# Attention scores in two PSUM tiles instead of one, with a new instruction order

## The chip, the cores and the metric

The kernel runs on one core of a Trainium2 chip. The metric is device time in microseconds (us) of one execution. The core has five engines with queues of their own, each in order: TensorE (PE; its weight loads are shown as PEld), VectorE (DVE), ScalarE (ACT), GpSimd (POOL) and SyncE (SP, which issues the DMAs here). Semaphores order the work between them. Matmul results go to PSUM, which DVE and ACT read.

## The reference

Causal attention with a compressive memory, then a feed-forward layer; B = 4, H = 8, S = 576, D = 64, 2304 tokens, d_model 512, d_ff 2048:

```python
scores = scale * np.matmul(q, k.transpose(0, 1, 3, 2))     # causal, softmax
local = np.matmul(a, v)
mem_out = np.einsum('bhsd,bhde->bhse', q_p, M_prev) / mem_norm
out = g * mem_out + (1 - g) * local
x = out.transpose(0, 2, 1, 3).reshape(B * S, H * D)
h = x @ w_in
g = np.maximum(h, 0.0) + alpha * np.minimum(h, 0.0)
return (g @ w_out).astype(np.float32)
```

## The kernel before

The work is written as calls on five engine objects of a class `Work`. `add` (L212) does not issue an instruction: it records it with its dependencies on earlier ones, found from the regions that it reads and writes. For PSUM the region is a mask of 512-column banks, made by `banks` (L206), so that two accesses of one tile in different banks get no edge. `issue` (L389) then ranks all recorded instructions, adds biases by phase and engine from the table `STAGES` (L32), lays them out against a table of costs (`lay`, L319), and issues them in the order of their planned starts, each on its engine's queue. The framework under the kernel sets the semaphores from that order and from the tiles that the instructions touch; the kernel has no say in them. All instructions go through one line, L417 (two matmuls issued as a pair: L242 and L243).

Queries come in five blocks of rows: 64 rows of all four batches together at first (batch "Z"), then four blocks of 128 rows of each batch, i = 1 to 4, each of which sees 64 + 128 i keys. A unit is one head with two blocks: a narrow unit has i = 1 and 2 (192 and 320 columns of scores), a wide one i = 3 and 4 (448 and 576). Per batch there are 8 narrow units and then 8 wide ones. A unit's scores are matmuls into PSUM (`unit_scores`, L959; in batches 1 to 3 two fp16 matmuls for each piece of up to 512 columns, with qT and then with qS, into the same place; 576 goes as 512 and 64). DVE reads each block once, with mask, scale and row maximum (`lowest`: E<-s, which also writes mx), ACT takes the exponential, `unit_probs` scales, splits into two fp16 parts (P) and transposes by DMA to PT, and `pair_values` multiplies with v into the tile bank. In batch 0 scores are fp32: `first_pair` (L930) runs two heads at once as paired matmuls, and the probabilities of narrow units are turned by TensorE in `unit_probs`, four blocks at a time, copied out by ACT (PT<-s). Between all of these TensorE runs the MoE matmuls (h for x @ w_in, y for g @ w_out), which make up most of its time; after the last unit it runs them alone.

PSUM has eight banks: one for the tile bank, two each for h and y, and three in one tile SS (name s in the profile) for scores:

- batch Z's scores and values, and the narrow units of batches 1 to 3 (both blocks in one bank): the next of three banks, by `third`
- wide units of batches 1 to 3: 448 in the first bank, 576 in the second and third
- batch 0: narrow pairs in the first two banks, one head each; turned blocks in the third; wide pairs with 448 in the third and 576 in the first two

Of the kernel before, what the change touches and what calls it, by code (L numbers as in the profile page):

```python
# [33 lines left out]
        "A0": -271.6, "A:DVE": -630.1, "BK0": 128.2, "BK:ACT": 57.8, "C0": -243.2, "C1": 111.2, "C2": -388.2,  # L34
        "C3": -1232.9, "C:ACT": 6.9, "C:DVE": -1010.6, "C:PE": -155.1, "I:DVE": 74.2, "I:POOL": 455.7,
# [9 lines left out]
        "P:DMA": -611.7, "P:DVE": -1203.9, "P:PE": -63, "P:POOL": 139.7, "S0": 5563.1, "S1": -1561.9, "S3": -1827.9,  # L45
        "S:ACT": 91.8, "S:DVE": 248, "V0": -1.2, "V:PE": -55.7, "a0": -645.8, "a1": -2.3, "a2": -2, "a3": 458.7,
        "a4": 395.9, "a:ACT": -1239, "a:DVE": -1609.6, "bk0": -153.9, "bk1": 135.1, "bk2": -2.6, "bk3": -1.5,
        "bk:ACT": -1438.9, "bk:DMA": -473.7, "bk:DVE": -477.6, "bk:PE": -584.5, "bv0": 174, "bv1": 65.7, "bv2": 2.6,
# [5 lines left out]
        "o31": -1071.1, "o33": -466.4, "o:ACT": -431.9, "o:DMA": 29.3, "o:DVE": -726.2, "o:PE": -469.3, "oZ": -11.6,  # L54
        "oZ:ACT": -1559.9, "oZ:DVE": -1291.2, "oZ:PE": -81.7, "p1": -2914.9, "p2": -286.9, "p3": -715.7, "p4": 13.8,
        "p:ACT": -1229.2, "p:DVE": -633.5, "q1": 61.7, "q2": -1110, "q3": 59, "q:ACT": -234.1, "q:DVE": -671.8,
# [7 lines left out]
        "y:DVE": -1121.7, "y:PE": 639.6,  # L64
    }),
# [4 lines left out]
        "C:ACT": -20.6, "C:DVE": -11.7, "C:PE": 37.9, "I": 6.7, "I:POOL": 1.3, "J": 1.8, "J:ACT": -11.3,  # L70
# [12 lines left out]
        "P33:DVE": 1.3, "P33:POOL": 14.4, "P:ACT": -9.2, "P:DMA": -16.7, "P:DVE": -12.2, "P:PE": 14.4, "P:POOL": 4.9,  # L83
# [6 lines left out]
        "bk:ACT": -23.9, "bk:DMA": 2, "bk:DVE": -13.2, "bk:PE": 28.8, "bv0:ACT": -10.3, "bv0:DVE": -13, "bv1": -0.4,  # L90
# [83 lines left out]
class Work:  # L174
# [31 lines left out]
    def banks(self, ap):  # L206

        (ps, pn), *free = ap.ap
        o = ap.offset % ps
        return (2 << (o + sum(st * (n - 1) for st, n in free)) // 512) - (1 << o // 512)  # L210
# [210 lines left out]
def kernel(  # L421
# [24 lines left out]
    NP = H // 2  # L446
# [28 lines left out]
    def third():  # L475
        turns[0] += 1
        return SS[:, turns[0] % 3 * 512:turns[0] % 3 * 512 + 512]
# [979 lines left out]
```

## Time and profile before

| | us |
|---|---|
| median of 3 runs (584.89 to 585.94) | 585.43 |
| the profiled execution | 584.66 |
| its span, first to last instruction | 582.8 |
| TensorE busy | 541.5 |
| DVE busy | 456.0 |
| ACT busy | 380.7 |

The mean granted clock of TensorE is 0.972 of 2.4 GHz. The profile shows, per engine, when each instruction ran, how long the engine sat idle before it, and which other engine's instruction released it ("<-"). Names are the program's, out<-in: s is the tile SS, E the scores after DVE, mx the row maxima.

### The profile page before, as it was taken

How to read it: one execution, taken by the hardware profiler on the slowest of the kernel's cores; microseconds unless marked ns; L12 is line 12 of the kernel's file. 1: busy time of each engine (PE TensorE's matmuls, PEld its weight loads, DVE VectorE, ACT ScalarE, POOL GpSimd, SP SyncE). 2: the span in 40 equal slices, each digit the busy share in tenths (PEclk: the TensorE clock that was granted, in tenths of full speed). 3: DMA queues.
4: the chain of work that ended last, by engine and by line, in shares of the span. 5: the costliest groups of instructions: out<-in, count | busy, mean ns of one | idle time of the engine just before them, and what ended most of it. 6: DMA issues, size and time to landing. Idle time of an engine off the chain costs nothing.

```text
span 582.8 us, 12013 instructions
## 1 busy us (share of the span) xinstructions
PE 541.5 (93%) x4421; PEld 356.6 (61%) x4421; DVE 456.0 (78%) x1197; ACT 380.7 (65%) x790; POOL 81.6 (14%) x142
## 2 busy tenths in 40 slices
PE   9558999799999999989899999999999899999997
PEld 4347644364566676647666767587666666766663
DVE  4898899789999899999999999989887664322331
ACT  3466696658989468978788787886886653322322
POOL 2000310031420021211222120221221110000000
PEclk9759999799999999999999999999999999999999
DMA  7899738563489795476998838788545470100000
GB/s 254 197 342 237 208 94 244 193 165 82 91 162 204 175 219 121 99 164 153 207 231 186 177 100 162 162 181 160 105 87 103 126 157 14 47 1 1 36 1 36
DMA packets 226026, 82.84 MB, mean 142 GB/s; under 512 B 216224, under 2 KB 216240, under 8 KB 225968
## 3 DMA queue, kind: packets, MB, share of 16 engines
q1 hardware_dynamic: 225968, 82.09, 60.1%
q8 instruction: 34, 0.56, 0.4%
q14 instruction: 24, 0.20, 0.1%
HBM read 35.66 MB, written 5.77 MB: 71 GB/s over the span
## 4 chain that ended last, share of the span: by engine, by line
PE 62%; DVE 16%; ACT 8%; issue 5%; DMA 5%; POOL 2%; SPq 2%; POOLq 0%; DVEq 0%; ACTq 0%
PE y L417 24%; PE h L417 24%; PE s L417 7%; PE bank L417 4%; DVE E L417 4%; DVE P L417 3%; POOL E L417 2%; DMA E<-in_moe_w_in_dram 2%; SPq L417 2%; DVE r L417 2%; DVE gg L417 1%; DVE R L417 1%; ACT r L417 1%; PE s L242 1%; ACT q L417 1%
## 5 line engine op out<-in xcount | busy, mean ns | idle before, releaser
L417 PE MATMUL h<-x,R 128*128 128x256 f16 x1536 | 256.2, 273 | 1.5 <-DVE r L417 1.4
L417 PE MATMUL y<-R,gg 128*128 128x512 f16 (+1 forms) x832 | 254.3, 397 | 1.3 <-ACT t L417 0.7
L417 PE MATMUL bank<-v,PT 128*128 128x64 f16 x1224 | 190.4, 193 | 0.1
L417 PEld LDWEIGHTS <-R 128*128 128x128 f16 x1536 | 148.8, 98 | 38.0 <-issue 6.3
L417 PEld LDWEIGHTS <-PT 128*128 128x128 f16 x1224 | 118.2, 98 | 19.3 <-issue 14.9
L417 PEld LDWEIGHTS <-gg 128*128 128x128 f16 x768 | 74.7, 98 | 76.6 <-issue 1.3
L417 POOL TENSOR_SCALAR E<-q,nrm,sm 128x64 f32<-128x64 f32 x112 | 69.0, 630 | 277.8 <-DVE sm L417 173.4
L417 ACT ACTIVATE E<-E,mx 128x320 f32<-128x320 f32 (+3 forms) x136 | 81.0, 601 | 30.1 <-DVE mx L417 26.1
L417 DVE SCALAR_TENSOR_TENSOR P<-E,mx,P 128x384 f16<-128x384 f32 (+3 forms) x112 | 75.4, 699 | 5.9 <-ACT P L417 5.3
L417 DVE SCALAR_TENSOR_TENSOR r<-r,oma,h 128x256 f32<-128x256 f32 x128 | 56.6, 475 | 26.8 <-ACT r L417 26.6
L417 ACT ACTIVATE P<-E,mx 128x384 f16<-128x384 f32 (+3 forms) x112 | 70.6, 673 | 10.0 <-POOL E L417 7.9
L417 ACT ACTIVATE r<-h 128x512 f32<-128x512 f32 x72 | 41.9, 589 | 50.7 <-PE h L417 29.1
L417 DVE SCALAR_TENSOR_TENSOR gg<-r,gsc,gg 128x512 f16<-128x512 f32 x56 | 41.8, 747 | 40.6 <-ACT gg L417 31.5
L417 DVE CUSTOM_DVE_ANT_0 E<-s,mask,pm 128x320 f32<-128x320 f32 (+3 forms) x96 | 57.4, 611 | 11.0 <-PE s L417 9.2
L417 ACT ACTIVATE gg<-r,gsc 128x512 f16<-128x512 f32 x56 | 40.0, 716 | 38.3 <-PE y L417 36.1
L417 PE MATMUL s<-k,qT 128*128 128x64 f16 (+5 forms) x136 | 36.4, 294 | 5.9 <-DVE mx L417 5.6
L417 PE MATMUL s<-k,qS 128*128 128x192 f16 (+4 forms) x120 | 32.7, 294 | 5.9 <-DVE mx L417 5.9
L417 PE MATMUL h<-R 128*128 128x256 f32 x128 | 31.4, 386 | 2.3 <-ACT R L417 1.9
L417 PEld LDWEIGHTS h<-R 128*128 128x128 f32 x128 | 22.9, 190 | 8.8 <-ACT R L417 2.7
L417 ACT ACTIVATION_READ_ACCUMULATOR E<-E,mx 128x1 f32 x124 | 23.3, 188 | 0.0
L417 ACT ACTIVATE R<-R,wsc 128x1024 f16<-128x1024 f32 x16 | 18.3, 1143 | 7.5 <-PE h L417 3.6
L417 ACT ACTIVATE t<-y,u 128x512 f32<-128x512 f32 x18 | 12.2, 680 | 13.2 <-PE y L417 13.0
(183 smaller groups left out, 628.5 us busy)
## 6 DMA issues: line engine op xcount, KB each, us to landing
q<-in_q_dram SPq DMA_DIRECT2D x16, 256.0 KB, 4.2
vn<-in_v_dram SPq DMA_DIRECT2D x16, 256.0 KB, 4.1
out_dram<-t SPq DMA_DIRECT2D x16, 256.0 KB, 2.3
kn<-in_moe_w_in_dram SPq DMA_DIRECT2D x6, 512.0 KB, 6.6
kn<-in_moe_w_out_dram SPq DMA_DIRECT2D x6, 512.0 KB, 4.7
kn<-in_k_dram SPq DMA_DIRECT2D x12, 256.0 KB, 3.9
qS<-qT SPq DMA_DIRECT2D x24, 128.0 KB, 2.6
R<-in_moe_w_in_dram SPq DMA_DIRECT2D x4, 512.0 KB, 6.6
```

The lines of the kernel that those rows point to most:

```text
L242: first[1](*first[2], **first[3])
L417: fn(*a, **kw)
```

## The change

SS becomes two tiles: s1 of one bank and s2 of two banks. The banks that are used are the same number; where they lie:

- batch Z and the narrow units of batches 1 to 3 alternate between s1 and the first bank of s2 (`other` in place of `third`)
- wide units of batches 1 to 3: 448 in s1, 576 in s2
- batch 0: narrow pairs in s2, turned blocks in s1; wide pairs with 448 in s1 and 576 in s2

`banks` goes; in the plan every access to a PSUM tile now counts as an access to the whole tile. The functions s1, s2, s3 are renamed, since the names are used for tiles. All values in STAGES are new, and so is the order that `issue` makes from them. The instructions are otherwise the same.

```diff
--- before.py
+++ after.py
@@ -31,106 +31,108 @@
 STAGES = [
     (2, {
-        "A0": -271.6, "A:DVE": -630.1, "BK0": 128.2, "BK:ACT": 57.8, "C0": -243.2, "C1": 111.2, "C2": -388.2,
-        "C3": -1232.9, "C:ACT": 6.9, "C:DVE": -1010.6, "C:PE": -155.1, "I:DVE": 74.2, "I:POOL": 455.7,
...
+        "A0": 10.6, "A:DVE": 50.6, "BK0": 102.5, "BK:ACT": -27.7, "BK:PE": 3.4, "C0": -56.4, "C1": 22.3, "C2": 335.8,
+        "C3": -920, "C:ACT": 1096.2, "C:DVE": -3.8, "C:PE": -943.6, "I": -699.2, "I:DVE": 79.2, "I:POOL": 497.7,
...
@@ -203,12 +205,6 @@
         m, size = self.known[key], ps * w
         return sum(m << size * h for h in range(2) if p0 < 64 * (h + 1) and p0 + pn > 64 * h), size
 
-    def banks(self, ap):
-
-        (ps, pn), *free = ap.ap
-        o = ap.offset % ps
-        return (2 << (o + sum(st * (n - 1) for st, n in free)) // 512) - (1 << o // 512)
-
     def add(self, kind, engine, name, a, kw):
         outs = [kw[x] for x in ("out", "accum_out") if kw.get(x) is not None]
         rest = list(a) + [x for n, x in kw.items() if n not in ("out", "accum_out")]
@@ -223,7 +219,7 @@
         for x, write in [(x, False) for x in ins] + [(x, True) for x in outs]:
             if x.tensor.name in self.fixed:
                 continue
-            m = self.banks(x) if x.space == PSUM else self.cells(x)[0]
+            m = 1 if x.space == PSUM else self.cells(x)[0]
             wrote, read = self.state.setdefault(x.tensor.name, ([], []))
             deps.update(o for o, c in wrote if c & m)
             if not write and x.space == PSUM:
@@ -469,12 +465,13 @@
 
     bank = psp.tile([128, 512], F32, tag="bank")
     o_sc = bank[:, 256:512]
-    SS = psp.tile([128, 1536], F32, tag="s")
+    s1 = psp.tile([128, 512], F32, tag="s1")
+    s2 = psp.tile([128, 1024], F32, tag="s2")
     turns = [0]
 
-    def third():
+    def other():
         turns[0] += 1
-        return SS[:, turns[0] % 3 * 512:turns[0] % 3 * 512 + 512]
+        return (s1, s2[:, 0:512])[turns[0] % 2]
     ident = cp.tile([128, 128], F32, name="ident")
     ones = cp.tile([128, 128], F32, name="ones")
     mask = cp.tile([128, 576], F32, name="mask")
@@ -936,8 +933,8 @@
             for a in range(2):
                 i = bl[j if bl[0] == 1 else a ^ j ^ 1]
                 w = 64 + 128 * i
-                o = 512 * a + 192 * j if bl[0] == 1 else 1024 if i == 3 else 0
-                cols.append((a, i, SS[:, o:o + w]))
+                o = 512 * a + 192 * j if bl[0] == 1 else 0
+                cols.append((a, i, (s1 if i == 3 else s2)[:, o:o + w]))
             cols.sort(key=lambda x: -x[2].shape[1])
             for c0 in (0, 512):
                 for n, (a, i, row) in enumerate(cols):
@@ -966,10 +963,10 @@
         width = [64 + 128 * i for i in bl]
         es, mx, sm = unit_tiles(b, h, bl)
         if bl[0] == 1:
-            ps = third()
+            ps = other()
             where = [ps[:, 0:width[0]], ps[:, width[0]:sum(width)]]
         else:
-            where = [SS[:, 0:width[0]], SS[:, 512:512 + width[1]]]
+            where = [s1[:, 0:width[0]], s2[:, 0:width[1]]]
         qT, qS, k1, _ = stacks[b, h // 2]
         for i, w, s in zip(bl, width, where):
             for c0 in range(0, w, 512):
@@ -1003,7 +1000,7 @@
             PT = wkp.tile([128, 9, 128], F32, tag="PT", bufs=TB)
             for c0 in range(0, ns, 4):
                 c1 = min(c0 + 4, ns)
-                pt = SS[:, 1024:1024 + 128 * (c1 - c0)]
+                pt = s1[:, 0:128 * (c1 - c0)]
                 for c in range(c0, c1):
                     T.transpose(pt[:, (c - c0) * 128:(c - c0) * 128 + 128], E[:, c * 128:c * 128 + 128], ident)
                 A.copy(PT[:, c0:c1].rearrange("p s c -> p (s c)"), pt)
@@ -1092,7 +1089,7 @@
                              (n["k"][t], [(ps, kT[ps, a]) for a, ps in enumerate((slice(0, 64), slice(64, 128)))], "y")):
             flipped([x[:, 2 * a:2 * a + 2].rearrange("p h d -> p (h d)") for a in range(NP)],
                     [(ps, o.rearrange("p n c -> p (n c)")) for ps, o in outs], tag)
-        s = third().rearrange("p (h n) -> p h n", h=H)
+        s = other().rearrange("p (h n) -> p h n", h=H)
         for h in range(H):
             for c in (slice(0, 64), slice(64, 128)):
                 T.matmul(s[c, h, :], lhsT=qT[:, h // 2, c], rhs=kT[:, h % 2, h // 2, c], start=True, stop=True)
@@ -1120,7 +1117,7 @@
         (V if OZ[0] else G).tensor_tensor(E, E, sm[:, :, None].to_broadcast([128, H, 64]), op=ALU.mult)
         PT = wkp.tile([128, H, 128], F32, tag="PT", bufs=TB)
         flipped([P[:, h] for h in range(H)], [(slice(0, 128), PT.rearrange("p h c -> p (h c)"))], "hy"[t])
-        o = third().rearrange("p (a n) -> p a n", a=NP)
+        o = other().rearrange("p (a n) -> p a n", a=NP)
         for h in range(H):
             a, ps = h // 2, slice(64 * (h % 2), 64 * (h % 2) + 64)
             for b in range(2):
@@ -1276,13 +1273,13 @@
     V.tensor_scalar(xsc, ra[:, 0, 0:1], XS * 2.0 ** -15, None, op0=ALU.mult)
     V.tensor_scalar(isa, ra[:, 1, 0:1], 2.0 ** 15, None, op0=ALU.mult)
 
-    def s1(u):
+    def scores(u):
         unit_scores(*u)
 
-    def s2(u):
+    def probs(u):
         unit_probs(*u)
 
-    def s3(u):
+    def values(u):
         b, h, bl = u
         if h % 2 == 1:
             if h == 1:
@@ -1305,7 +1302,7 @@
     def tick():
         t = done[0]
         done[0] += 1
-        for f, lag in ((s3, LAG), (s1, 0), (s2, 1)):
+        for f, lag in ((values, LAG), (scores, 0), (probs, 1)):
             if 0 <= t - lag < len(units) and units[t - lag]:
                 f(units[t - lag])
         do(bulk[:BULK])
```

## Rows read from the trace of the kernel before

**Rows 1.** The page: busy time by engine; the chain that ended last, by engine and line.
```profile
PE 541.5 (93%) x4421; PEld 356.6 (61%) x4421; DVE 456.0 (78%) x1197; ACT 380.7 (65%) x790; POOL 81.6 (14%) x142
...
PE 62%; DVE 16%; ACT 8%; issue 5%; DMA 5%; POOL 2%; SPq 2%; POOLq 0%; DVEq 0%; ACTq 0%
PE y L417 24%; PE h L417 24%; PE s L417 7%; PE bank L417 4%; DVE E L417 4%; DVE P L417 3%; POOL E L417 2%; DMA E<-in_moe_w_in_dram 2%; SPq L417 2%; DVE r L417 2%; DVE gg L417 1%; DVE R L417 1%; ACT r L417 1%; PE s L242 1%; ACT q L417 1%
```

**Rows 2.** Windows: length; busy us (count) of PE, PEld, DVE, ACT, POOL; clock; DMA share, GB/s.
```profile
0.00:60.00 60.00, 42.91 (x286) 28.75 (x288) 47.43 (x126) 31.00 (x77) 4.22 (x13) 0.80 0.92 257
60.00:120.00 60.00, 54.21 (x241) 29.78 (x242) 51.72 (x160) 43.10 (x106) 7.89 (x16) 0.94 0.63 187
...
180.00:480.00 300.00, 286.67 (x2793) 198.45 (x2790) 268.49 (x715) 228.09 (x478) 52.49 (x96) 1.00 0.73 155
480.00:583.00 103.00, 99.14 (x706) 63.62 (x703) 31.81 (x62) 29.66 (x46) 0.00 (x0) 0.99 0.07 22
```

**Rows 3.** Waits of the whole span: us in total, times, longest.
```profile
PE s L417 <- DVE mx L417: 11.5, 22, 0.8
...
DVE E L417 <- PE s L417: 9.4, 17, 1.0
...
PE s L417 <- ACT PT L417: 2.4, 4, 0.8
```

**Rows 4.** Timeline, TensorE, 248 to 262: start, duration, instruction, [idle before, releaser].
```profile
250.25 0.35 PE L417 MATMUL s<-k,qS 128*128 128x448 f16 x1 [0.64 <-DVE mx L417]
...
254.38 0.35 PE L417 MATMUL s<-k,qT 128*128 128x448 f16 x1
...
261.91 0.19 PE L417 MATMUL s<-k,qS 128*128 128x64 f16 x1 [0.75 <-DVE mx L417]
```

**Rows 5.** Timeline, DVE, the same stretch.
```profile
249.37 0.82 DVE L417 CUSTOM_DVE_ANT_0 E<-s,mask,pm 128x576 f32<-128x576 f32 x1
...
254.78 0.82 DVE L417 CUSTOM_DVE_ANT_0 E<-s,mask,pm 128x576 f32<-128x576 f32 x1 [0.41 <-PE s L417]
...
261.17 0.68 DVE L417 CUSTOM_DVE_ANT_0 E<-s,mask,pm 128x448 f32<-128x448 f32 x1 [0.44 <-PE bank L417]
```

**Rows 6.** Chain of waits, 248 to 262: start, us, what.
```profile
249.37 0.82 DVE E L417
```

**Rows 7.** Groups by form: count, busy us, mean ns, idle before, releasers.
```profile
L417 PE MATMUL s<-k,qS 128*128 128x448 f16 x24 | 8.4, 352 | 3.3 <-DVE mx L417 3.3
...
L417 PE MATMUL s<-k,qT 128*128 128x64 f16 x24 | 4.6, 192 | 2.9 <-DVE mx L417 2.9
...
L417 PE MATMUL s<-k,qS 128*128 128x64 f16 x24 | 4.6, 192 | 1.5 <-DVE mx L417 1.5
...
L417 PE MATMUL s<-k,qS 128*128 128x512 f16 x24 | 9.1, 379 | 0.8 <-DVE mx L417 0.8
...
L417 PE MATMUL s<-k,qS 128*128 128x320 f16 x24 | 7.0, 299 | 0.3 <-DVE mx L417 0.3
```

**Rows 8.** Tile s, 188 to 214; then timeline of TensorE and DVE to 224.
```profile
L417 PE MATMUL s<-k,qT x8: 246/272/300, 191.8 to 213.7; 128*128 128x192 f16 x4, 128*128 128x320 f16 x4
L417 PE MATMUL s<-k,qS x8: 244/272/300, 191.9 to 209.7; 128*128 128x192 f16 x4, 128*128 128x320 f16 x4
L417 DVE CUSTOM_DVE_ANT_0 E<-s,mask,pm x6: 413/480/550, 200.9 to 212.9; 128x320 f32<-128x320 f32 x3, 128x192 f32<-128x192 f32 x3
...
213.66 0.25 PE L417 MATMUL s<-k,qT 128*128 128x192 f16 x1
...
222.37 0.30 PE L417 MATMUL s<-k,qT 128*128 128x320 f16 x1 [0.31 <-DVE mx L417]
...
221.78 0.53 DVE L417 CUSTOM_DVE_ANT_0 E<-s,mask,pm 128x320 f32<-128x320 f32 x1
...
222.95 0.42 DVE L417 CUSTOM_DVE_ANT_0 E<-s,mask,pm 128x192 f32<-128x192 f32 x1 [0.63 <-PE s L417]
```

**Rows 9.** Timeline, TensorE, a transpose of batch 0's turned blocks.
```profile
86.82 0.33 PE L417 MATMUL s<-ident,E 128*128 128x128 f32 x1 [0.68 <-ACT PT L417]
```

More of the change, by code (lines that the diff above doesn't have):

```diff
@@ L33 @@
     (2, {
-        "A0": -271.6, "A:DVE": -630.1, "BK0": 128.2, "BK:ACT": 57.8, "C0": -243.2, "C1": 111.2, "C2": -388.2,
-        "C3": -1232.9, "C:ACT": 6.9, "C:DVE": -1010.6, "C:PE": -155.1, "I:DVE": 74.2, "I:POOL": 455.7,
[9 rows of a table removed]
-        "P:DMA": -611.7, "P:DVE": -1203.9, "P:PE": -63, "P:POOL": 139.7, "S0": 5563.1, "S1": -1561.9, "S3": -1827.9,
-        "S:ACT": 91.8, "S:DVE": 248, "V0": -1.2, "V:PE": -55.7, "a0": -645.8, "a1": -2.3, "a2": -2, "a3": 458.7,
-        "a4": 395.9, "a:ACT": -1239, "a:DVE": -1609.6, "bk0": -153.9, "bk1": 135.1, "bk2": -2.6, "bk3": -1.5,
@@ L48 @@
-        "bk:ACT": -1438.9, "bk:DMA": -473.7, "bk:DVE": -477.6, "bk:PE": -584.5, "bv0": 174, "bv1": 65.7, "bv2": 2.6,
[5 rows of a table removed]
-        "o31": -1071.1, "o33": -466.4, "o:ACT": -431.9, "o:DMA": 29.3, "o:DVE": -726.2, "o:PE": -469.3, "oZ": -11.6,
-        "oZ:ACT": -1559.9, "oZ:DVE": -1291.2, "oZ:PE": -81.7, "p1": -2914.9, "p2": -286.9, "p3": -715.7, "p4": 13.8,
-        "p:ACT": -1229.2, "p:DVE": -633.5, "q1": 61.7, "q2": -1110, "q3": 59, "q:ACT": -234.1, "q:DVE": -671.8,
[7 rows of a table removed]
-        "y:DVE": -1121.7, "y:PE": 639.6,
+        "A0": 10.6, "A:DVE": 50.6, "BK0": 102.5, "BK:ACT": -27.7, "BK:PE": 3.4, "C0": -56.4, "C1": 22.3, "C2": 335.8,
@@ new lines @@
+        "C3": -920, "C:ACT": 1096.2, "C:DVE": -3.8, "C:PE": -943.6, "I": -699.2, "I:DVE": 79.2, "I:POOL": 497.7,
+        "J:ACT": 470.6, "J:DVE": 108, "J:PE": -179.3, "K": 47.5, "K:POOL": 2.3, "L0K": -713.8, "L0K:DMA": 228.2,
[6 rows of a table added]
+        "LW:DMA": 605.3, "LZ": 27.3, "LZ:DMA": -1145.9, "Lz": 8.5, "Lz:DMA": -8.6, "N": 87.9, "N:PE": 292.5,
+        "P01": 4, "P03": 3.7, "P11": 777.2, "P13": 823.4, "P21": 168.1, "P23": 236.6, "P31": -675.3, "P33": -247.2,
+        "P:ACT": 988.7, "P:DMA": 668.5, "P:DVE": -882.6, "P:PE": -157.8, "S0": 4737.2, "S1": -1253, "S3": -2953.6,
@@ new lines @@
+        "S:ACT": -87.5, "S:DVE": 168.1, "V0": -874.8, "V:DVE": 211.2, "V:PE": -90.8, "a0": 5.7, "a1": 46.8,
+        "a2": -161.5, "a3": 389.6, "a4": -42.9, "a:ACT": -265.2, "a:DVE": 239.4, "bk0": -173.5, "bk1": 344.8,
+        "bk2": 244.5, "bk3": 3.1, "bk:ACT": -687.5, "bk:DMA": 246.9, "bk:DVE": 1380.7, "bk:PE": 100.3, "bv0": -0.7,
[5 rows of a table added]
+        "o31": 144.8, "o33": 10.1, "o:ACT": -779.8, "o:DMA": 580.1, "o:DVE": -613.6, "o:PE": 33.3, "oZ": 10.8,
[5 rows of a table added]
+        "v:DVE": 634.9, "v:PE": 331.4, "x0": -121.5, "x:ACT": 2.1, "x:DVE": 73.7, "y0_10": -412.5, "y0_11": -68.6,
@@ L65 @@
+        "y0_30": 187.3, "y0_31": 1834.4, "y1_10": -18.1, "y1_11": 103.3, "y1_30": -419.6, "y1_31": 103.8,
+        "y2_10": 184.2, "y2_11": 220.2, "y2_30": -3073.8, "y2_31": -122.6, "y3_10": 764.1, "y3_11": 98,
+        "y3_31": 447.3, "y4_11": -1599.1, "y:ACT": -1231.1, "y:DMA": 642.8, "y:DVE": -750.7, "y:PE": 1282.7,
     }),
     (1, {
[3 rows of a table removed]
-        "C:ACT": -20.6, "C:DVE": -11.7, "C:PE": 37.9, "I": 6.7, "I:POOL": 1.3, "J": 1.8, "J:ACT": -11.3,
[12 rows of a table removed]
-        "P33:DVE": 1.3, "P33:POOL": 14.4, "P:ACT": -9.2, "P:DMA": -16.7, "P:DVE": -12.2, "P:PE": 14.4, "P:POOL": 4.9,
[6 rows of a table removed]
@@ L90 @@
-        "bk:ACT": -23.9, "bk:DMA": 2, "bk:DVE": -13.2, "bk:PE": 28.8, "bv0:ACT": -10.3, "bv0:DVE": -13, "bv1": -0.4,
[12 rows of a table removed]
-        "h4_11:DVE": -11.2, "h4_11:PE": 46.8, "h:ACT": -8.7, "h:DVE": -12.2, "h:PE": 45.7, "n": 4, "n:PE": 0.2,
[5 rows of a table removed]
-        "o33:PE": 1.8, "o:ACT": -22.9, "o:DMA": -16.1, "o:DVE": -13.2, "o:PE": 46, "oZ": 3.1, "oZ:ACT": 0.2,
[9 rows of a table removed]
-        "s33:PE": 48.3, "s:ACT": 6, "s:DVE": -12.2, "s:PE": 45.5, "sZ": 7.1, "sZ:DVE": -0.4, "sZ:PE": 0.3,
[13 rows of a table removed]
-        "y:DVE": -11.7, "y:PE": 45.5,
[3 rows of a table added]
+        "C3:PE": -8.9, "C:ACT": 13.2, "C:DVE": 9.3, "C:PE": -17.2, "I": -57.9, "I:POOL": -8.6, "J:ACT": -18.7,
[6 rows of a table added]
@@ new lines @@
+        "LW3": -8.7, "LW3:DMA": -22.1, "LW:DMA": -2.8, "LZ:DMA": -42.6, "Lz:DMA": -4.4, "N": 0.9, "N:PE": -13.7,
[5 rows of a table added]
+        "P33:DMA": -3.8, "P33:DVE": -7.4, "P33:POOL": -37, "P:ACT": 15, "P:DMA": -20.1, "P:DVE": 8.9, "P:PE": -86.4,
[21 rows of a table added]
+        "h4_11:PE": -16.7, "h:ACT": 10, "h:DVE": 8.9, "h:PE": -16.3, "n": -27.5, "n:PE": -9.4, "o01": -15,
[5 rows of a table added]
+        "o33:DVE": 21.3, "o33:PE": -55.2, "o:ACT": -0.5, "o:DMA": -50.1, "o:DVE": 13.1, "o:PE": -18, "oZ": -97,
[4 rows of a table added]
+        "q:ACT": 39, "q:DVE": 9.7, "r0:ACT": 0.9, "r0:DVE": 9.9, "r:ACT": 35.7, "r:DVE": 13.6, "s01:ACT": -1.2,
[4 rows of a table added]
@@ L134 @@
+        "s33:ACT": 1.7, "s33:PE": -49.1, "s:ACT": 12.1, "s:DVE": 8.9, "s:PE": -16.3, "sZ": 8.1, "sZ:ACT": 98.3,
[14 rows of a table added]
+        "y4_11:PE": -16, "y:ACT": 21.9, "y:DMA": 2.5, "y:DVE": 8.4, "y:PE": -16.3,
     }),
```

159 rows, old and new, of the table STAGES are left out of this document.

## The prediction

> **What bounds the kernel now.** I read the page first. TensorE is busy 541.5 of 582.8 us, and it has 62% of the chain that ended last; DVE has 16%, and its reads of the scores (DVE E) are 4% of the span [rows 1]. So an idle microsecond of TensorE counts nearly in full, as long as its backlog of MoE matmuls only moves forward. Second, the windows by stretch say where TensorE idles: 17.1 us in 0 to 60 (60 less 42.91), 5.8 in 60 to 120, 13.3 in 180 to 480 and 3.9 in 480 to 583, the last a stage in which it runs almost alone [rows 2]. From 180 us on the granted clock is 1.00, the 2.4 GHz level, so time saved there has no second price in clock. Third, the waits: "PE s <- DVE mx" is 11.5 us in 22 waits, by far the largest wait of TensorE, and on the other side DVE waits 9.4 us in 17 pieces for score matmuls [rows 3].
>
> What these 11.5 us are is the core of the case. A wide unit writes 448 columns into bank 0 and 576 (512 and 64) into banks 1 and 2 of the one tile SS. DVE starts reading the 576 at 249.37 for 0.82 us [rows 5]; the second matmul of the 448, in another bank, starts only at 250.25, after 0.64 us of idle, put down to that read [rows 4]. The first matmul of the same 448 columns has already run, so bank 0 was free: nothing in the data asks for this wait. The other direction shows too: at 254.38 TensorE begins another first matmul of a 448, which lasts 0.35, and DVE's read of the 576 starts at 254.78, 0.05 after its end, with 0.41 of idle [rows 4, 5]. A third pair is the 448 read at 261.17 and the 64-column matmul at 261.91, 0.75 late. The semaphores therefore go by tile here, not by bank. The chain of waits runs through such a read (0.82 us of DVE at 249.37), so it is on the path [rows 6]. The planner of before does not know: its `banks` gives accesses in different banks no edge, so it lays the matmul beside the read and the chip puts it behind.
>
> **The Trainium skill against the trace.** "PSUM — Partial Sum Buffer", section "PSUM bank collisions raise a hardware error", says that engines on different banks run clean and that a guard by bank is enough. By this rule the three banks of SS need no waits between them, splitting the tile would save nothing, and the sum would stay at the time before. The measurement differs: the 448's matmul waited 0.64 us on a read in other banks [rows 4, 5]. I go by the rows; the rule's outcome is a rival below.
>
> **The change, part by part.**
>
> *Wide units of batches 1 to 3.* The blocks keep their banks' count, but lie in two tiles, s1 (448) and s2 (512 and 64). Waits between them go. By form of matmul, TensorE's idle time before 448 of qS is 3.3, before 64 of qT 2.9, before 64 of qS 1.5, before 512 of qS 0.8 and before 320 of qS 0.3 us [rows 7]: 8.8 us. All of these are later matmuls of a block whose first one has been written, so their own place was free. I count all as saved. The other 2.7 us (11.5 less 8.8) stand before first matmuls, which may have to wait for a read of their own place; I take half, 1.3, with ends 0 and 2.7. DVE's 9.4 us of waiting for scores [rows 3] also shrink, at no price: DVE has 31.5 us of idle time in 180 to 480 [rows 2], so when TensorE moves forward by 10 us there, DVE is still not full. I add nothing for it, since TensorE sets the end.
>
> *Narrow units of batches 1 to 3.* Before, they rotate over three banks, after over two tiles, with the second bank of s2 unused. This is the change's cost. In 188 to 214 us four pairs of 320-column matmuls are done, and two more units have begun (the last at 213.66), while DVE has read three units [rows 8]. The sixth unit thus stands in the place of the third. In a rotation of two it has to wait for the fourth's reads, which end at 223.37: 9.7 us later. So the third place is used, and up to 18 units (six of eight in each batch) are pushed back. But DVE's reading is what is late: the scores of such a unit lie unread for many microseconds, and what was written early was not read earlier. Queued behind a score matmul on TensorE are the MoE matmuls, which have nothing to do with it; the new order, whose planner has the two tiles as they are, can put them in front. The cost is bounded below by 0 (a gain beyond that is in the sum already) and above by both reads of a unit, 0.53 and 0.42 us [rows 8], for all 18: 17.1 us. The nearest measured case of a narrow score behind a read is 0.31 us at 222.37 [rows 8]. I take that for every third unit: 6 x 0.31 = 1.9 us.
>
> *Batch 0.* Narrow pairs write both banks of s2 as they wrote banks 0 and 1, and turned blocks have one bank as before. The wait of transposes for ACT's copies, 2.4 us [rows 3], as 0.68 at 86.82 [rows 9], is a true one between two users of one bank, and stays. That pairs and turned blocks no longer wait for each other is worth little: no PE wait of that kind over 0.3 us is among the rows I found. 0, with 1 as the end. The wide pairs write 448 and 576 together; a pair needs both reads either way: 0. Scores and values of the first blocks go from three places to two, and each use is read before the next but one: 0.
>
> *`banks` removed, `m = 1`.* This adds edges only in the plan, where the chip has waits already. It costs no instruction. Renamed functions: 0.
>
> *New order.* Same instructions, other queue order on every engine, SP's loads and POOL's included. The trace of before can't show it. I bound it by idle time that an order can win or lose: TensorE's 17.1 + 5.8 us before 120 us [rows 2]. A quarter of that either way is 5.7 us; I take 0, as the loads and warm-up that fill this stage are the same.
>
> **Sum.** The profiled execution took 584.66 us (582.8 of span, 1.9 around it), 0.77 below the median of 585.43. 584.66 - 8.8 - 1.3 + 1.9 = 576.5; with 0.77 that is 577.2 us at the median, 1.4% less. With the order's 5.7 either way: 571.5 to 582.9.
>
> **Rivals.**
>
> *The wait is not the tile's (same).* If the semaphores go by bank, and the rows show a chance meeting of waits, the split saves nothing and the time is 585.4, give or take 1. Against it: three pairs within 13 us, each ending within 0.15 us of the other engine's instruction, in both directions [rows 4, 5]. Likewise if DVE becomes the bound and takes all back. Against that: its 31.5 us of idle time. Together 0.13.
>
> *Two places for narrow scores bind (slower).* The place is the narrow stage of batches 1 to 3, where TensorE stands before a score, with MoE matmuls queued behind, until DVE has read the unit before the last. At the full price, 585.4 - 8.8 + 17.1 = 593.7. It decides from 8.8 / 18 = 0.49 us a unit on: below, the change still gains. For it: the third place is in use throughout [rows 8]. Against it: TensorE waited only 0.31 where it met such a read, and the planner sees the two tiles. 0.13.
>
> *More than the false waits (faster still).* If the first matmuls' waits go too and the order wins half of the idle time in 60 to 120: 585.4 - 11.5 - 2.9 = 571.0. 0.12.
>
> The forecast holds the remaining 0.62.
>
> **How the numbers follow.** Time 577.2. The range must reach the order's ends and the case without a saving: 570 to 586 leaves out the slow rival and the far end of the fast one, under 0.2 together. Within 0.2% means 584.3 to 586.6, about what a measurement of this kernel can tell from none. Faster: 0.62 + 0.12 + 0.04 (the part of the first rival in which a little is left) = 0.78; same 0.09; slower 0.13.
>
> **What would show it.** Right: "PE s <- DVE mx" falls from 11.5 to 3 us or less, no 448 or 64 of qS or 64 of qT waits for DVE any more, TensorE's idle time in 180 to 480 falls from 13.3 to about 5, and a read of 576 runs beside a 448 matmul. The buffers' price shows as waits before narrow 192-column first matmuls, each ended by DVE; over 0.49 us on average means the slow rival. Wrong: the same waits at the same places (waits not by tile); or idle time that moves ahead of 120 us or to "PE bank <- DMA" and "PE h <- DVE" (new order); or waits gone and the end unmoved, with DVE without idle time in 180 to 480.

## The result and the profile after

The changed kernel takes 562.77 us (median of 4 runs, 561.1 to 564.0) against 585.16 before: a ratio of 0.961, 95% interval 0.959 to 0.964, so 22.4 us less. The forecast was 577.2, its range 570 to 586; the direction held, the time lies below the range. Its profiled execution took 562.94 us, 561.1 of it span; before, 584.66 and 582.8.

The page of the changed kernel, to be read against [rows 1]: busy time by engine, and the chain that ended last by engine and by line.

```profile
PE 533.8 (95%) x4421; PEld 353.8 (63%) x4421; DVE 452.7 (81%) x1197; ACT 377.9 (67%) x790; POOL 84.8 (15%) x142
...
PE 54%; DVE 8%; DMA 5%; issue 2%; ACT 1%; POOL 0%; POOLq 0%; DVEq 0%
PE y L413 24%; PE h L413 22%; PE bank L413 4%; PE s L413 4%; DMA PT<-P 4%; DVE P L413 2%; DVE E L413 1%; DVE q L413 1%; DVE r L413 1%; DMA k<-k 1%; DVE nrm L413 1%; DVE t L413 1%; DVE gg L413 1%; DMA x<-xn 1%; ACT P L413 0%
```

TensorE works the same 4421 matmuls in 7.7 us less (541.5 to 533.8) and is idle 14.0 us less (582.8 less 541.5 is 41.3; 561.1 less 533.8 is 27.3). The chain's shares add up to 70% of the span here and to all of it before, so they can't be set beside each other as they stand; of the part that was followed DVE has 8 in 70, and its reads of scores (DVE E) 1 in 70, against 16 and 4 in 100 before.

The windows of the changed kernel, with the columns of [rows 2]:

```profile
0.00:60.00 60.00, 46.88 (x314) 30.73 (x315) 48.83 (x137) 34.82 (x87) 4.27 (x13) 0.89 0.93 257
60.00:120.00 60.00, 59.17 (x271) 34.76 (x268) 58.58 (x174) 47.42 (x113) 13.65 (x20) 1.00 0.69 195
120.00:180.00 60.00, 58.97 (x511) 36.57 (x510) 58.66 (x133) 53.48 (x91) 11.62 (x13) 1.00 0.60 134
180.00:480.00 300.00, 291.37 (x2813) 202.78 (x2811) 261.69 (x707) 219.16 (x465) 55.23 (x96) 0.99 0.73 153
480.00:562.00 82.00, 77.36 (x523) 48.94 (x519) 24.92 (x49) 22.97 (x36) 0.00 (x0) 0.99 0.06 22
```

Idle time of TensorE by stretch, before to after: 17.1 to 13.1 in 0 to 60, 5.8 to 0.8 in 60 to 120, 13.3 to 8.6 in 180 to 480. So 9.0 of the 14.0 us of idle time that went lay ahead of 120 us, where my sum had 0; and there the granted clock rose from 0.80 to 0.89 and from 0.94 to 1.00, between the levels of 1.2 and 2.4 GHz.

What TensorE waits for now (us in total, times, longest), the four longest:

```profile
PE bank L413 <- DVE stv L413: 4.8, 1, 4.8
PE bank L413 <- DMA PT<-P: 4.7, 5, 1.4
PE h L413 <- DVE P L413: 3.4, 1, 3.4
PE h L413 <- DMA x<-xn: 2.4, 1, 2.4
```

"PE s <- DVE mx", 11.5 us in [rows 3], is not in this list at all, and none of its rows names a score matmul that waits for DVE. By form the idle time before the later matmuls of a block, 8.8 us in [rows 7], is zero, and so is that before DVE's reads of narrow units:

```profile
L413 DVE CUSTOM_DVE_ANT_0 E<-s,mask,pm 128x320 f32<-128x320 f32 x24 | 13.0, 543 | 0.0
...
L413 DVE CUSTOM_DVE_ANT_0 E<-s,mask,pm 128x192 f32<-128x192 f32 x24 | 9.9, 411 | 0.0
...
L413 PE MATMUL s<-k,qS 128*128 128x512 f16 x24 | 9.1, 380 | 0.0
...
L413 PE MATMUL s<-k,qS 128*128 128x448 f16 x24 | 8.5, 353 | 0.0
...
L413 PE MATMUL s<-k,qS 128*128 128x320 f16 x24 | 7.0, 299 | 0.0
...
L413 PE MATMUL s<-k,qT 128*128 128x64 f16 x24 | 4.6, 193 | 0.0
...
L413 PE MATMUL s<-k,qS 128*128 128x64 f16 x24 | 4.6, 193 | 0.0
```

The timeline shows the pair of [rows 4] and [rows 5] as it runs now. First TensorE, the two matmuls of a 448, then DVE, the read of a 576, all of the changed kernel:

```profile
250.01 0.35 PE L413 MATMUL s<-k,qT 128*128 128x448 f16 x1
...
250.23 0.35 PE L413 MATMUL s<-k,qS 128*128 128x448 f16 x1
```

```profile
249.77 0.81 DVE L413 CUSTOM_DVE_ANT_0 E<-s,mask,pm 128x576 f32<-128x576 f32 x1
```

Both matmuls run inside the read (249.77 to 250.58) and nobody waits. In the whole trace 11 of the 32 reads of a 576 have a score matmul beside them. In the trace before no read of the tile by DVE or ACT overlaps a matmul into it, whatever the banks.

### The profile page after: what moved, and what is told of

Its sections match the earlier page's. It is cut to its first block, busy times and chain, and to the rows that moved or that the text cites. A ratio compares the mean times of both kernels' runs of the same rounds, so it can differ in the third digit from the quotient of the medians.

```text
span 561.1 us, 12018 instructions
## 1 busy us (share of the span) xinstructions
PE 533.8 (95%) x4421; PEld 353.8 (63%) x4421; DVE 452.7 (81%) x1197; ACT 377.9 (67%) x790; POOL 84.8 (15%) x142
## 4 chain that ended last, share of the span: by engine, by line
PE 54%; DVE 8%; DMA 5%; issue 2%; ACT 1%; POOL 0%; POOLq 0%; DVEq 0%
PE y L413 24%; PE h L413 22%; PE bank L413 4%; PE s L413 4%; DMA PT<-P 4%; DVE P L413 2%; DVE E L413 1%; DVE q L413 1%; DVE r L413 1%; DMA k<-k 1%; DVE nrm L413 1%; DVE t L413 1%; DVE gg L413 1%; DMA x<-xn 1%; ACT P L413 0%
## 5 line engine op out<-in xcount | busy, mean ns | idle before, releaser
L413 PE MATMUL h<-x,R 128*128 128x256 f16 x1536 | 263.8, 274 | 2.5 <-DMA x<-xn 2.4
L413 PE MATMUL y<-R,gg 128*128 128x512 f16 (+1 forms) x832 | 260.0, 398 | 0.7 <-DVE C L413 0.7
L413 PE MATMUL bank<-v,PT 128*128 128x64 f16 x1224 | 182.9, 193 | 5.6 <-DMA PT<-P 4.7
L413 PEld LDWEIGHTS <-PT 128*128 128x128 f16 x1224 | 114.5, 98 | 15.2 <-DMA PT<-P 7.8
L413 POOL TENSOR_SCALAR E<-q,nrm,sm 128x64 f32<-128x64 f32 x112 | 70.7, 644 | 317.5 <-DVE sm L413 256.1
L413 ACT ACTIVATE P<-E,mx 128x384 f16<-128x384 f32 (+2 forms) x112 | 70.9, 674 | 14.1 <-POOL E L413 7.4
L413 DVE SCALAR_TENSOR_TENSOR P<-E,mx,P 128x384 f16<-128x384 f32 (+2 forms) x112 | 76.0, 699 | 5.3 <-ACT P L413 4.9
L413 DVE CUSTOM_DVE_ANT_0 E<-s,mask,pm 128x320 f32<-128x320 f32 (+2 forms) x96 | 56.8, 610 | 3.0 <-PE s L413 3.0
L413 PE MATMUL s<-k,qT 128*128 128x64 f16 (+5 forms) x136 | 37.8, 294 | 1.5 <-DMA k<-k 1.5
L413 DVE SCALAR_TENSOR_TENSOR R<-R,wsc 128x1024 f16<-128x1024 f32 x16 | 20.4, 1275 | 0.2 <-ACT R L413 0.2
```

The lines of the kernel that those rows point to most:

```text
L413: fn(*a, **kw)
```

## The experiments

Each kernel ran on the same chip as runs of the kernel before, whose median there was 584.2 to 585.3 us. The chips are not the same for all: h5, z1 and z2 ran on a second one and z4 on a third, so the ratios to the kernel before are the safer comparison between them and the rest. The tile split and the order were parted first by holding one of them to the instruction.

### Tiles and order, each with the other held

`e1_one_tile`: the new order on every engine, the scores in one tile again. The plan still treats the two parts as two tiles, so that the order doesn't move.

```diff
-    s1 = psp.tile([128, 512], F32, tag="s1")
-    s2 = psp.tile([128, 1024], F32, tag="s2")
+    SS = psp.tile([128, 1536], F32, tag="s")
+    s1, s2 = SS[:, 1024:1536], SS[:, 0:1024]
...
+            if key.startswith("s_0"):
+                key += "12"[x.offset % x.ap[0][0] < 1024]
```

> The new order, instruction for instruction, with the scores back in one tile of three banks (s2 is its first 1024 columns, s1 its last 512); only the waits can differ from the changed kernel. Theory (waits go by tile): waits of TensorE on DVE's reads (PE s <- DVE mx) come back, 9 to 12 us, and the time is 572 to 575 us against 562.8. Rival (the order brings the gain, and the chance meetings with it): 562 to 565 us, and PE s <- DVE mx under 3 us.

Measured: 577.5 us, ratio to before 0.984 (0.981 to 0.988), so 14.7 us slower than the changed kernel with the same queues. Its waits in both directions:

```profile
DVE E L416 <- PE s L416: 10.3, 17, 3.5
...
PE s L416 <- DVE mx L416: 9.7, 20, 0.9
```

The rival falls: the order doesn't avoid the waits, it needs two tiles to be free of them. The loss is more than the 9.7 us that TensorE waits, and above the range that was expected. Its windows, and then its wait for DVE's reads in 180 to 480 alone and that of the kernel before in the same stretch:

```profile
0.00:60.00 60.00, 43.32 (x274) 27.46 (x275) 43.77 (x117) 30.65 (x75) 4.28 (x13) 0.83 0.92 242
60.00:120.00 60.00, 56.70 (x271) 31.95 (x270) 54.95 (x171) 46.14 (x113) 9.15 (x16) 1.00 0.65 190
...
180.00:480.00 300.00, 286.35 (x2736) 197.67 (x2735) 262.25 (x700) 219.94 (x465) 53.31 (x92) 0.99 0.73 153
```

```profile
PE s L416 <- DVE mx L416: 7.6, 16, 0.9
```

```profile
PE s L417 <- DVE mx L417: 11.1, 20, 0.8
```

At the units of batches 1 to 3 the new order in one tile thus has fewer false waits than the old one. What it loses beyond them, it loses early: by 120 us TensorE has run 545 matmuls, against 585 in the changed kernel, and has idled 20.0 us against 14.0, though only 2.1 of the 9.7 us lie there. Why the start is so much slower stays open; the profiled execution, 580.3 us, is also 2.9 above the median of its runs.

`e2_two_tiles`: the old order on every engine, the scores in s1 and s2. Narrow units rotate over s1 and both banks of s2, three places as before.

```diff
-    SS = psp.tile([128, 1536], F32, tag="s")
+    s1 = psp.tile([128, 512], F32, tag="s1")
+    s2 = psp.tile([128, 1024], F32, tag="s2")
...
-            where = [SS[:, 0:width[0]], SS[:, 512:512 + width[1]]]
+            where = [s1[:, 0:width[0]], s2[:, 0:width[1]]]
```

> The old order, instruction for instruction, with the scores in two tiles of one and two banks (narrow units still rotate over three banks). Theory (waits go by tile): the 8.8 to 11.5 us of TensorE's waits before later matmuls of a block go, and the time is 574 to 577 us against 585.2; the remaining 11 to 14 us to the changed kernel are the new order's. Rival (waits not by tile, all is order): 584 to 586 us.

Measured: 575.1 us, ratio 0.982 (0.979 to 0.986), 10.2 less than before and within what was expected. Its busy time, and of its waits a new one and the two that answer to [rows 3]:

```profile
PE 538.6 (94%) x4421; PEld 355.4 (62%) x4421; DVE 453.7 (79%) x1197; ACT 379.6 (66%) x790; POOL 81.3 (14%) x142
```

```profile
PE bank L424 <- DMA PT<-P: 3.1, 4, 1.6
...
PE s L424 <- ACT PT L424: 2.4, 4, 0.8
...
PE s L424 <- DVE mx L424: 1.7, 5, 0.6
```

"PE s <- DVE mx" falls from 11.5 to 1.7 with the queues untouched; the 2.4 us of transposes behind ACT stay, as they are waits for one bank. Its windows:

```profile
0.00:60.00 60.00, 43.84 (x293) 29.17 (x294) 47.56 (x127) 31.15 (x77) 4.23 (x13) 0.83 0.92 257
60.00:120.00 60.00, 54.28 (x240) 30.11 (x239) 52.50 (x161) 43.48 (x107) 7.90 (x16) 0.94 0.64 192
120.00:180.00 60.00, 58.11 (x405) 35.32 (x404) 56.18 (x136) 49.98 (x87) 17.03 (x17) 1.00 0.61 126
180.00:480.00 300.00, 293.61 (x2876) 203.47 (x2875) 268.83 (x720) 228.90 (x480) 52.12 (x96) 1.00 0.74 155
```

The gain is where the waits were: idle time in 180 to 480 falls from 13.3 to 6.4 us, and ahead of 120 us all but 1.0 of it stays (16.2 and 5.7, against 17.1 and 5.8). So of 22.4 us 10.2 are the tiles' in the old order, and 12.3 the order's in two tiles; the other way round, 7.8 the order's in one tile and 14.7 the tiles'. The two ways differ by 4.4 us, or by 3.2 if the ratios are taken. As the interval of each ratio is some 2 us to either side, this is hardly clear of noise: that tiles and order help each other is likely, but not shown.

### The table with the other plan

`e4_old_table`: the changed kernel with the old values in STAGES. `e5_new_table`: the kernel before with the new ones. The edit is the table alone:

```diff
-STAGES = [(2, {"A0": 10.6, "A:DVE": 50.6, ...
+STAGES = [(2, {"A0": -271.6, "A:DVE": -630.1, ...
```

> The changed kernel (two tiles, plan by whole tile) with the old table of biases. If knowing the true waits is enough for the plan, 563 to 570 us; if the table has to be made for the plan, 575 to 590 us, since the order differs from both kernels' in many places.

> The kernel before (one tile, plan by bank) with the new table of biases. If the table alone carries the gain, 563 to 570 us. If tiles and plan carry it, 580 to 590 us, with PE s <- DVE mx at 9 us or more.

Measured: 595.5 us (ratio 1.017, 1.013 to 1.020) and 614.8 us (1.049, 1.046 to 1.053), both slower than was expected of either theory. Either table did worse with the other plan than with its own. The false waits are not what makes the difference: e4, with two tiles, has 1.6 us of them, and in e5 they are more than ever, but only 3.7 us more than before, of 29.5 us in time. The row of e5:

```profile
PE s L419 <- DVE mx L419: 15.2, 26, 1.4
```

### Without a table

To see what the plan is worth by itself, STAGES was emptied: `z1_new_no_table` (the changed kernel), `z2_old_no_table` (the kernel before) and `z4_one_tile_no_table` (the order of z1, held as in e1, with one tile).

```diff
-STAGES = [(2, {...}), (1, {...})]
+STAGES = [(2, {}), (1, {})]
```

> The changed kernel (two tiles, plan by whole tile) with an empty table, so that the order is the planner's own. With z2_old_no_table it tells what tiles and a plan that knows the waits are worth without a table made for either: theory (tiles 10 to 15 us, and a truer plan some more) 10 to 25 us faster than z2_old_no_table; rival (the plan's truth is worth nothing by itself): within 10 us of it.

> The kernel before (one tile, plan by bank) with an empty table. Both theories: slower than before by 20 us or more, 605 to 650 us, and by theory with over 11 us in PE s <- DVE mx; by the rival no more than 10 us slower than z1_new_no_table.

> The order of z1_new_no_table, instruction for instruction, with the scores in one tile of three banks. Without any table it parts the 17.7 us between z2_old_no_table (587.2) and z1_new_no_table (569.4). If the tiles are all of it: 585 to 589 us. If the tiles are worth what they were in the two tabled orders, 10 to 15 us, and a plan that counts by tile the rest: 579 to 584 us. If the plan is most of it: under 577 us.

Measured: z1 569.4 us (ratio 0.973, 0.969 to 0.977), z2 587.2 (1.004, 1.002 to 1.006), z4 585.1 (1.001, 0.999 to 1.004). The difference of z2 and z1, 17.7 us, is within what the theory had; that z2 would lose 20 us or more by losing its table was wrong, it loses 2.7 or so. z4, at the lower edge of what was expected if the tiles are all of it, parts the difference. It has the order and the places of z1, whose plan takes the scores for two tiles. They are worth 2.1 us (1.6 by the ratios) while there is one tile, which the intervals hardly tell from nothing, and the second tile is worth 15.6 us (16.5 by the ratios) in that order. The wait rows of z2 and of z4, one tile each:

```profile
PE s L314 <- DVE mx L314: 11.2, 17, 1.6
```

```profile
PE s L311 <- DVE mx L311: 11.6, 20, 0.9
```

In one tile z4 has as many false waits as z2. A plan that counts the one tile as one, and so knows of them, was not run; whether it could plan them away is not shown. In two tiles the order of z1 has none of them, and is by itself 5.7 us faster than the old order with its table (569.4 against 575.1 of e2). The new table adds 6.7 (569.4 to 562.8). These two make up the order's 12.3.

### Where the order's 12.3 us are won

These kernels take both orders as lists and follow the new one up to a cut, then the old one for what is left (h2 the other way round). All have two tiles.

```diff
-            for i in sorted(range(len(ops)), key=lambda i: (start[i], i)):
+            front = new[:cut]
+            has = set(front)
+            for i in list(front) + [i for i in old if i not in has]:
```

> Two tiles, narrow units over three banks as in e2_two_tiles. The queues follow the new order up to its first fp16 score (at 202 us in the changed kernel) and the old order for all that is left. Theory (what the order brings is all won before batch 1): 562 to 566 us, close to the changed kernel's 562.8. Rival (the order's gain lies in the middle and the tail): 572 to 576 us, close to e2_two_tiles' 575.1.

> The reverse: two tiles, narrow units over two places as in the changed kernel, the old order up to its first fp16 score (176 us) and the new order for the rest. Theory (gain before batch 1): 573 to 577 us. Rival (gain in the middle and the tail, or two places for narrow units as a cost that only the new order hides): 563 to 568 us, or over 580 us.

> As h1_front_new, but the new order only up to batch 0's first pair of scores (55.6 us in the changed kernel, 59.0 with the old order and two tiles). If the start (loads, warm-up, batch Z) brings it: 563 to 567 us. By the first pair's time it is about 3 us of the 12.3: 571 to 573 us.

> As h1_front_new, but the new order up to batch 0's first wide pair (101.0 us in the changed kernel, 115.5 with the old order and two tiles). If the start and batch 0's narrow units bring it: 562 to 566 us. If the weights and wide units of 101 to 202 us have a share: 567 to 573 us.

| new order | us | ratio to before, 95% |
|---|---|---|
| nowhere (e2) | 575.1 | 0.982 (0.979 to 0.986) |
| to batch 0's first pair (h3) | 572.4 | 0.978 (0.974 to 0.982) |
| to batch 0's first wide pair (h4) | 569.5 | 0.974 (0.969 to 0.978) |
| to batch 1's first score (h1) | 570.7 | 0.976 (0.973 to 0.980) |
| with all of batch 1's narrow units (h5) | 563.7 | 0.963 (0.958 to 0.967) |
| from batch 1's first score on (h2) | 580.8 | 0.994 (0.991 to 0.997) |
| everywhere | 562.8 | 0.961 (0.959 to 0.964) |

h3 and h4 came out as one of their theories had it; h1 lies between the two of its own. h2 is just over the 580 us of its rival's second form, two places for narrow units as a cost that only the new order hides; but its trace doesn't have the sign of that: the only waits of scores for DVE's reads are 0.4 us at batch 0's pairs. h1's trace says why it fell short. By 180 us TensorE has run 1063 matmuls (301, 276 and 486 in the three stretches of 60), against 938 in e2 and 1096 in the changed kernel. Then comes the seam. The windows of h1, and the wait that stands in them:

```profile
180.00:200.00 20.00, 18.48 (x148) 12.74 (x145) 18.91 (x40) 9.13 (x14) 0.00 (x0) 1.00 0.98 208
200.00:220.00 20.00, 13.53 (x79) 8.81 (x77) 12.27 (x38) 8.81 (x23) 1.53 (x4) 0.74 0.83 190
```

```profile
PE s L306 <- DMA k<-k: 5.0, 2, 2.8
```

In 200 to 220 TensorE idles 6.5 us, and the clock of that stretch falls to 0.74: e2 issues DMA transposes of batch 1's keys at 167.6 and 174.3 us, ahead of its first scores at 176; behind the new front of h1 they come at 196.9 and 200.9, and the old rest issues the scores at once. So I moved the cut behind batch 1's narrow units:

> Two tiles; the new order up to and with all of batch 1's narrow units (two places for them, as in the changed kernel), then the old order (three places in batches 2 and 3). In h1_front_new TensorE had done at 200 us as much as in the changed kernel, 12 us ahead of the old order, and lost 10 of them from 200 to 220, behind transposes for batch 1 (PE s <- DMA k<-k 5.0 us). Theory (the seam gave it back; the gain is made before 200 us and keeps if batch 1's preparation comes in the new order too): 562 to 566 us. Rival (the new front borrows from work that must be done later, and the old rest can't carry it): 569 to 573 us again.

Measured: 563.7 us, within what the theory had and 0.9 from the changed kernel. The same windows of h5:

```profile
180.00:200.00 20.00, 17.97 (x148) 12.20 (x146) 18.78 (x38) 9.58 (x14) 0.00 (x0) 1.00 0.94 202
200.00:220.00 20.00, 20.00 (x171) 14.85 (x169) 19.52 (x56) 14.26 (x34) 4.98 (x8) 1.00 1.09 224
```

No idle time in 200 to 220. So all of the 12.3 us but 0.9, which the intervals don't tell from nothing, are won by the end of batch 1's narrow units, and behind this front the new order of the rest brings nothing that these runs can show. By h3 and h4 some 5.6 of them are won before batch 0's wide units. How the other 6.7 split over batch 0's wide units and batch 1's start these cuts don't tell, since a seam costs too.

One such place can be read directly, the turn from batch 0's narrow to its wide units. Windows of e2 and then of the changed kernel:

```profile
100.00:110.00 10.00, 7.00 (x35) 3.29 (x33) 8.43 (x28) 8.08 (x21) 0.00 (x0) 0.95 0.68 229
110.00:120.00 10.00, 9.55 (x38) 5.73 (x39) 5.73 (x13) 5.21 (x11) 0.00 (x0) 0.71 0.65 180
```

```profile
100.00:110.00 10.00, 10.00 (x47) 6.18 (x47) 9.48 (x27) 7.06 (x14) 0.00 (x0) 1.00 0.83 222
110.00:120.00 10.00, 10.00 (x40) 7.43 (x40) 9.98 (x25) 7.29 (x14) 4.36 (x4) 1.00 0.46 135
```

With the old order TensorE idles 3.5 us in these 20, DVE and ACT are half idle in the second ten, and the clock falls to 0.71. In the new order TensorE has no gap, DVE is busy 19.5 of 20 and the clock stays at 1.00.

h2 doesn't tell what its rest costs. Its queues and places are e2's up to the cut, yet its profile, of the slowest of its runs, is behind e2's from 40 us on. The stretch 40 to 50 of h2 and of e2:

```profile
40.00:50.00 10.00, 7.96 (x74) 6.95 (x75) 10.00 (x17) 3.23 (x7) 0.00 (x0) 0.50 1.05 328
```

```profile
40.00:50.00 10.00, 7.82 (x88) 6.62 (x88) 10.00 (x12) 5.45 (x11) 0.00 (x0) 0.79 0.94 272
```

The clock is at the lower level for all of these ten us in one, and for a part of them in the other. From 576.7 to 584.7 us is also the widest spread of all these kernels, over 10 runs. Why its start ran slower isn't settled. It has a seam as well: in 180 to 200 TensorE is busy 15.5 of 20 us at a clock of 0.83, against 18.6 at 1.00 in e2. That the new rest gains nothing behind the old front is all that I take from it.

## Why the prediction was wrong, point by point

*The waits go by tile.* Right, and shown by e1, e2 and z4: queues held, tile split or joined. In e1 and z4 no read of a score tile has a matmul into it beside it, as before; in e2 11 of the 32 reads of a 576 have one, as in the changed kernel. The sign of the result and the rows that should vanish follow from it.

*Wide units: 8.8 and 1.3 us.* Right in mechanism, and in size for the old order: 10.1 in the sum, 10.2 measured in e2, and TensorE's wait for DVE 11.5 to 1.7. That the two sizes meet so closely is in part luck. TensorE's idle time fell by only 7.5 us (41.3 to 33.8), since waits for transposes came up (PE bank <- DMA PT<-P, 3.1 us in e2, not among the waits before), and its busy time fell by 2.9 (541.5 to 538.6), which the sum did not have. In the new order the same split is worth 14.7. The windows of e1's profile put the surplus ahead of 120 us, where the sum had 0 for the tiles, and not at the wide units. One sign missed too: TensorE's idle time in 180 to 480 was to fall to about 5 us; it is 6.4 in e2 and 8.6 in the changed kernel.

*Narrow units over two places: 1.9 us.* Too high. In the changed kernel no narrow score waits for DVE, and DVE's reads of them have 0.0 of idle time before them. That a third place was in use before [rows 8] didn't mean that it was needed: h5, with three places in batches 2 and 3, is not faster than the changed kernel with two (563.7 and 562.8 us). So the slower rival, which hung on this price, had nothing to stand on.

*Batch 0's transposes behind ACT: "stays".* It stays in e2 (2.4 us), as argued. In the changed kernel it is gone, with the same single bank, and so it is in e1: a true wait can be hidden by what the order puts in front of it.

*New order: 0, at most 5.7 either way.* This is the step that failed, and it alone carries the time out of the range: it brought 12.3 us in two tiles. Two things were wrong in it. I bounded it by a quarter of the idle time ahead of 120 us, with no row for the quarter; the order took 7.9 us there, from 21.9 in e2 to 14.0. I left out the clock, which I had dismissed for 180 us on only, though [rows 2] show it at 0.80 and 0.94 before that; the same matmuls take 538.6 us in e2 and 533.8 in the changed kernel, 4.8 less, with the clock up from 0.83 and 0.94 to 0.89 and 1.00 in the first two stretches. The 7.9 and the 4.8 us, less the 1.4 us by which the idle time behind 120 us grew, are the whole 11.3 us between the spans of the two profiled executions. Whether order and tiles are terms that can be added, as I took them to be, the runs leave open. "The loads and warm-up that fill this stage are the same" was true and beside the point: DVE was busy 52.5 of the 60 us from 60 to 120 in e2, and it is 58.6 now, so there was work to put into the gaps.

How much of the 4.8 us is the clock's can be bounded. These are the stretches at the lower level (0.50, 1.2 GHz) in e2 and then in the changed kernel:

```profile
23.70:44.20 20.50, 11.23 (x89) 9.10 (x89) 19.74 (x90) 11.81 (x45) 0.00 (x0) 0.50 0.97 298
109.00:115.80 6.80, 5.58 (x22) 2.71 (x22) 3.66 (x5) 3.15 (x8) 0.00 (x0) 0.50 0.38 128
```

```profile
31.00:44.70 13.70, 6.39 (x30) 5.24 (x32) 13.70 (x42) 6.40 (x20) 0.00 (x0) 0.50 1.04 343
188.00:191.40 3.40, 3.40 (x14) 1.96 (x14) 3.40 (x8) 0.00 (x0) 0.00 (x0) 0.50 0.88 209
```

TensorE works 16.8 us at it in e2 and 9.8 in the changed kernel. By the ratio of the two levels at most half of these 7.0 us is saved, so 3.5 us is an estimate of the clock's part from above; what saved the other 1.3 is not shown. That the order raises the clock is no chance of one profile: the mean granted clock is 0.984 to 0.988 in the four runs of the changed kernel and 0.970 to 0.976 in those of e2.

*The Trainium skill's rule.* "PSUM — Partial Sum Buffer", section "PSUM bank collisions raise a hardware error": guarding by bank is enough. The changed kernel agrees that engines on different banks can run at once (the 448 of s1 inside the read of s2). What the rule doesn't reach is which guards a program gets: in one tile they cover all of its banks, 11.5 us of waits before and none after.

*The faster rival*, at 0.12, had the right mechanism (first matmuls' waits gone too, idle time ahead of 120 us won) and would have given 571.0; it too left out the clock, and its gain from the order, 2.9 us, was a quarter of the real one.

## What to carry to other kernels

If one engine's write waits for another's read in a different bank of the same tile, make the banks tiles of their own, and price this by the waits before accesses whose own place is free; here that gave 10.1 us against 10.2 measured, in part by luck. If the same change lets a planner make a new order, don't put that at zero: price the idle time and the slow clock of every stretch where some engine has work left, and don't count on the two to add. A table of biases tuned for one plan was worse here than none for the other (614.8 against 587.2 us, 595.5 against 569.4).

## What was not expected of the hardware

The same queues can start at different speed: with the same old order in the queues up to far beyond it, the stretch 40 to 50 us ran at a granted clock of 0.79 in e2 and 0.50 in h2. TensorE is half idle just before (4.4 of 10 us busy in 30 to 40 in e2). With the new order it was 0.89 over the first 60 us of the changed kernel and 0.83 in e1, whose queues are equal too, though its tile is not. So the clock of such a start isn't the same from profile to profile, and a price for it taken from one profile is rough.
